# A fused attention and phase-mixing kernel on one core: the loads of the first batch, the angle reduction and the written-out order are changed

## The chip, the cores and the metric

The kernel runs on one core of one Trainium2 chip, in one launch. The metric is the device time of that core in microseconds. Five instruction streams take part: PE (TensorE, matmuls; PEld is its weight load), DVE (VectorE), ACT (ScalarE), POOL (GpSimd) and SP (SyncE, which only issues transfers). SP, ACT and POOL each have a queue of DMA transfers; all queues feed the same 16 DMA engines.

## The reference

The inputs `q`, `k`, `v` are 8 batches x 8 heads x 576 positions x 64 channels in float32. Attention without a softmax is followed by a normalisation, and its result `x` (8 x 576 x 512) goes through a layer that mixes positions with two 576 x 576 matrices and channels with one 512 x 512 matrix:

```python
kv = np.einsum('bhsd,bhse->bhde', k, v)
out = np.einsum('bhsd,bhde->bhse', q, kv)
x = out / sqrt(mean(out * out, axis=-1) + 1e-06) * g_norm    # heads side by side
theta = x @ w_theta
yr = np.einsum('ts,bsd->btd', w_tok_r, x * cos(theta))
yi = np.einsum('ts,bsd->btd', w_tok_i, x * sin(theta))
u = x + yr + yi
return u + np.maximum(u @ w_ch, 0.0)
```

## The kernel before, in words

The 576 positions of a batch are cut into four row tiles of 128 (j = 0 to 3) and a tail of 64 (j = 4), whose two halves of the channels lie above each other so that it fills 128 partitions with half the width. For each batch `b` the work is a chain of small tasks, each of one engine, and each has a short name in the code:

- loads of `k`, `v` (float32, into two buffers each, `kt` and `vt`) and of `q` (cast to float16 on the way, three buffers); each has a part of 512 positions ("heads", rows of 1 KB) and a part of the last 64 ("tail", rows of 256 bytes);
- `kv`: the products of k and v over all positions (L266, 80 small float32 matmuls a batch), copied into block-diagonal `kbd` (`ko`, L286 on ACT or L288 on DVE); `qt`, `qo`: q transposed;
- `raw` (L323), its squares on ACT (`sq`, L345), their sums on DVE (`ss`, L354), the root on POOL (`rt`, L364; for batch 0 on ACT and DVE), `x` on DVE (L386), `xt`, `xc`: x transposed and scaled by g;
- `th` (L451): theta into PSUM. The weights were scaled by 8/(2 pi) in advance, so that theta comes in eighths of a turn. Then `pt` (`whole_turns`, ACT, L467) adds a large number that rounds theta to whole turns; `ar` (`reduce_arg`, DVE, L472) takes the difference to theta, with theta read from PSUM; `ab` (`even_arg`) takes its absolute value (ACT, L480, or DVE on the bits as int32, L482); `si` (L490) and `co` (L497) are the sine of the difference and, by the absolute value and a quarter turn as bias, the cosine, each 512 wide on ACT;
- `z` (DVE, L520; the tail L509): x times both, 1024 wide, into `zm`;
- `y` (L543): the mixing of positions, 8 column tiles in 3 parts each, with weights `wT` that are made once at the start from `w_tok_i` and `w_tok_r` (`wt`: transposes on PE, `wo`: copies); `um` (DVE, L548): u; `ut`, `uo`: u transposed back; `v` (L451): u @ w_ch; `fin` (DVE, L585): the output tile; `st`: its store, from SP.

Nothing is looped at run time, and nothing is scheduled by the framework. `TURNS` is a table of task numbers; `play` walks it and emits each task, so each engine executes its own tasks in the table's order and waits, in order, for what each needs. A `*` picks the second of two engines that a task may run on; `r6` or `a20` are so many idle matmuls on PE (L623), which do no useful work. A queue's transfers start in the order of its issuing engine, and an instruction that waits on SP or POOL holds up all that stands behind it there.

At the start, SP loads k of batch 0, g and theta's weights (float32, into the space of `zm[1]`; four `wg` tasks, three on ACT and one on DVE, scale them into float16 `wth`), then v and k of batch 1. ACT loads v of batch 0. POOL loads q of batch 0, then waits by a one-element copy (`hold`, L232) until the second half of k has landed, loads the two token matrices, waits in the same way for v of batch 1, and loads q of batches 1 and 2 and `w_ch`.

## Time and profile before

| what | value |
|---|---|
| median of 3 runs (lowest, highest) | 214.74 us (213.78, 215.28) |
| the profiled execution: span, first to last instruction | 212.2 us |
| mean granted TensorE clock | 0.988 |
| busy: PE, DVE, ACT, POOL | 199.3, 177.7, 137.2, 75.7 us |
| read from and written to HBM | 33.06 MB, 9.44 MB |

The profiled execution's own time is not listed beside its span; the span lies 2.5 us under the median of the runs (214.74 - 212.2), and that difference stands for what lies around it. Of a row in a view of groups: the line, engine and operation, what it writes and reads, its shape, how often (x), then busy time in us, mean ns of one, and the idle time in front. PE's busy time overlaps from one matmul to the next, so a PE that is busy all the time may still do less than it could.

### The profile page before, as it was taken

What the parts mean: (1) busy time and instruction counts of PE and PEld (TensorE: products, weight loads), DVE (VectorE), ACT (ScalarE), POOL (GpSimd) and SP (SyncE); (2) the same over time, 40 slices, a digit from 0 to 9 for tenths busy, and PEclk for the clock granted to TensorE, in tenths of its full rate; (3) what the DMA queues carried; (4) which work ended last, traced back from release to release, by engine and by line L of the source; (5) the groups of instructions that cost most, each with busy time, mean ns of one, the idle gap of its engine ahead of it and who ended that gap; (6) DMA issues with size and microseconds to landing.
All of it is one profiled execution on the core that took longest, in us unless ns stands there. A gap on an engine that the chain in (4) does not pass through costs nothing.

```text
span 212.2 us, 5401 instructions
## 1 busy us (share of the span) xinstructions
PE 199.3 (94%) x2152; PEld 137.2 (65%) x2152; DVE 177.7 (84%) x379; ACT 137.2 (65%) x268; POOL 75.7 (36%) x74
## 2 busy tenths in 40 slices
PE   7699699999999999989999999999999999999992
PEld 2246368886766785857776567867567856665850
DVE  6007998979999989999999998877997999899652
ACT  2006798658993776845999878574765998466030
POOL 6400070058814750654874550313325630400000
PEclk9889999999999999999999999999999999999998
DMA  6999999993999993999989928956583587563315
GB/s 202 269 298 245 246 249 191 303 313 103 131 226 357 287 240 77 240 229 238 287 259 224 227 29 223 321 140 175 140 183 94 145 121 228 123 90 124 111 55 170
DMA packets 68712, 41.98 MB, mean 198 GB/s; under 512 B 37584, under 2 KB 63824, under 8 KB 68688
## 3 DMA queue, kind: packets, MB, share of 16 engines
q1 hardware_dynamic: 53440, 33.89, 62.0%
q0 software_dynamic: 13664, 6.57, 23.6%
q10 hardware_dynamic: 1584, 1.18, 1.8%
q8 instruction: 17, 0.28, 0.5%
...
HBM read 33.06 MB, written 9.44 MB: 200 GB/s over the span
## 4 chain that ended last, share of the span: by engine, by line
PE 50%; DVE 31%; DMA 7%; ACT 4%; POOL 4%; issue 3%; DVEq 0%; POOLq 0%; ACTq 0%
PE y L543 19%; PE th L451 8%; PE v L451 6%; DVE ot L585 5%; PE kv L266 5%; DVE ss L354 5%; DVE arg L472 4%; POOL rt L364 4%; DVE zm L520 4%; DMA vt<-in_v_dram 3%; DVE zt L509 3%; PE idle L623 3%; DVE x L386 3%; DVE wn L548 2%; DVE kbd L288 2%
## 5 line engine op out<-in xcount | busy, mean ns | idle before, releaser
L364 POOL TENSOR_TENSOR rt<-ss,mhalf 128x8 f32<-128x8 f32 (+1 forms) x35 | 53.6, 1537 | 85.3 <-DVE ss L354 85.0
L543 PE MATMUL y<-wT,zm 128*128 128x320 f16 (+1 forms) x512 | 78.5, 286 | 1.7 <-DVE zm L520 0.9
L543 PEld LDWEIGHTS <-zm 128*128 128x128 f16 x512 | 48.1, 98 | 18.3 <-issue 2.6
L548 DVE SCALAR_TENSOR_TENSOR wn<-y,gcol,xT 128x320 f16<-128x320 f32 (+1 forms) x64 | 31.4, 511 | 2.8 <-PE y L543 2.6
L451 PE MATMUL th<-wth,xT 128*128 128x512 f16 x128 | 32.2, 379 | 0.8 <-DVE kbd L288 0.8
L467 ACT ACTIVATE arg<-th 128x512 f32<-128x512 f32 (+1 forms) x40 | 21.7, 552 | 16.2 <-PE th L451 15.6
L451 PE MATMUL v<-wch,wn 128*128 128x512 f16 x128 | 31.7, 379 | 0.0
L497 ACT ACTIVATE sc<-arg,quarter 128x512 f16<-128x512 f32 (+1 forms) x40 | 26.4, 672 | 0.8 <-DVE arg L482 0.7
L472 DVE SCALAR_TENSOR_TENSOR arg<-arg,th 128x512 f32<-128x512 f32 (+1 forms) x40 | 24.9, 628 | 1.4 <-ACT arg L467 1.3
L490 ACT ACTIVATE sc<-arg 128x512 f16<-128x512 f32 (+1 forms) x40 | 22.9, 583 | 4.3 <-DVE arg L472 4.2
L386 DVE TENSOR_TENSOR x<-raw,rt 128x512 f16<-128x512 f32 x32 | 21.8, 685 | 3.9 <-POOL rt L364 3.5
L266 PE MATMUL kv<-vt,kt 128*64 128x64 f32 x640 | 21.2, 224 | 2.0 <-DMA vt<-in_v_dram 2.0
L354 DVE TENSOR_REDUCE ss<-sqb 128x8 f32<-128x520 f32 x32 | 21.8, 687 | 0.9 <-ACT sqb L345 0.7
L345 ACT ACTIVATE sqb<-raw 128x512 f32<-128x512 f32 x32 | 18.6, 597 | 6.1 <-PE raw L323 5.9
L266 PEld LDWEIGHTS kv<-vt,kt 128*64 128x64 f32 x640 | 19.7, 138 | 4.1 <-issue 2.9
L520 DVE TENSOR_TENSOR zm<-x,sc 128x1024 f16<-128x1024 f16 x32 | 21.7, 685 | 0.6 <-ACT sc L497 0.5
L585 DVE SCALAR_TENSOR_TENSOR ot<-v,us 128x512 f32<-128x512 f32 (+1 forms) x28 | 16.8, 609 | 3.3 <-PE v L451 2.6
L451 PEld LDWEIGHTS <-wn 128*128 128x128 f16 x128 | 11.9, 98 | 10.8 <-issue 0.2
L451 PEld LDWEIGHTS <-xT 128*128 128x128 f16 x128 | 11.7, 98 | 10.8 <-issue 1.4
L543 PE MATMUL y<-wT,zt 128*128 128x320 f16 (+1 forms) x64 | 18.3, 286 | 0.1
L286 ACT COPY us<-ups 128x512 f16<-128x512 f16 (+1 forms) x16 | 8.6, 542 | 13.2 <-PE ups L281 11.7
L480 ACT ACTIVATE arg<-arg 128x512 f32<-128x512 f32 (+1 forms) x25 | 14.1, 575 | 2.8 <-DVE arg L472 2.8
...
## 6 DMA issues: line engine op xcount, KB each, us to landing
...
vt<-in_v_dram SPq DMA_DIRECT2D x7, 1024.0 KB, 9.7
kt<-in_k_dram SPq DMA_DIRECT2D x7, 1024.0 KB, 9.8
...
kt<-in_k_dram SPq DMA_DIRECT2D x8, 128.0 KB, 8.6
zm<-in_moe_w_theta_dram SPq DMA_DIRECT2D x1, 1024.0 KB, 11.7
```

The costliest lines, as they stand in the source:

```text
L266: nc.tensor.matmul(t[i * D:(i + 1) * D, hp - lo, :], ks, vs, start=(hp == lo and j == 0), stop=(hp == lo + n - 1 and j == NT - 1),)
L354: nc.vector.reduce_sum(out=ss[:], in_=sq_sb.pop((b, j))[:], axis=AXX)
L364: nc.gpsimd.tensor_tensor(out=rt[:], in0=ss[:], in1=mhalf[:, 0:h], op=ALU.pow)
L386: nc.vector.tensor_tensor(out=x_pair[b, p][:, :, a * HC:(a + 1) * HC].rearrange("p t (h e) -> p h t e", e=D), in0=r[:].rearrange("p (h t e ...
L451: nc.tensor.matmul(t[:], piece(kc), w[:, kc, :], start=first, stop=last)
L472: nc.vector.scalar_tensor_tensor(out=arg[:, 0, :], in0=arg[:, 1, :], scalar=MAGIC, in1=th_ps.pop((b, j))[:], op0=ALU.subtract, op1=ALU.sub ...
L490: nc.scalar.activation(out=sc[:, 0, :], in_=arg_sb[b, j][:, 0, :], func=AFT.Sin, bias=0.0, scale=-TURN * SHRINK,)
L497: nc.scalar.activation(out=sc_sb[b, j][:, 1, :], in_=arg_sb.pop((b, j))[:, 1, :], func=AFT.Sin, bias=quarter[:], scale=-TURN * SHRINK,)
L520: nc.vector.tensor_tensor(out=dst, in0=x.unsqueeze(1).broadcast_to((P, 2, w)), in1=sc[:], op=ALU.mult)
L543: nc.tensor.matmul(t[:, 0:hi - lo], s, wT[:, w, lo:hi], start=n == 0, stop=n == len(z) - 1)
L548: nc.vector.scalar_tensor_tensor(out=uTb[b % NUT][:, c, lo:hi], in0=y_ps.pop((b, h, c))[:, 0:hi - lo], scalar=gcol[:, 0:1], in1=xTb[b % NX ...
L585: nc.vector.scalar_tensor_tensor(out=ot[:].rearrange("p (c s) -> p c s", s=P), in0=v_ps.pop((b, j))[:].rearrange("p (c s) -> p c s", s=P), ...
```

## The change

1. Batch 0's v goes on SP's queue too, and the order there is first half of v, first half of k, both tails, second halves. A `hold` can now stand anywhere in the table (`p` on POOL: a one-element copy; `s` on SP: a one-element transfer); it reads an element of a loaded buffer (`landed`), so the issuing engine waits for that load before it issues the next. There are 12 on POOL and 8 on SP.
2. Theta's weights are loaded by POOL with a cast to float16, unscaled. The staging in `zm[1]` and the four `wg` tasks go.
3. The angle: `pt` (`turns`, ACT) writes theta times 2^20/(2 pi) as int32; `pq` (`quarter_on`) writes the same plus a quarter turn beside it, on ACT from PSUM (25 of 40) or on DVE from the first half (15); `ar` (`wrap`, DVE) shifts both halves left by 12 bits in one instruction of 1024 int32, which drops whole turns; `si` (`sines`, ACT) takes one sine of 1024. `ab` and `co` go.
4. A store may go on POOL's queue: 11 full tiles and 6 tail halves do. There are four output buffers instead of three.
5. `TURNS` is new throughout, with new choices of engine: of the 36 instructions of `ko`, 4 instead of 18 are on DVE (the others on ACT), of the full `qo` 2 instead of 8; of the full `xc`, 10 instead of 5 are on DVE, of the full `xo` 3 instead of 1. Idle matmuls: 28 instead of 36.

SP's queue from its start (`kt`, `vt` are the buffers of k and v, with the buffer's number; 128x4x256 is one half of the heads, 64x8x64 the tail). Before:

```order
L187 DMA kt0_64<-in_k_dram 128x4x256 x2
L229 DMA gcol_102<-in_g_norm_dram 64x1
L193 DMA kt0_64<-in_k_dram 64x8x64
L229 DMA gcol_102<-in_g_norm_dram 64x1
L223 DMA zm1_77<-in_moe_w_theta_dram 128x4x512
L187 DMA vt1_67<-in_v_dram 128x8x256
L193 DMA vt1_67<-in_v_dram 64x8x64
L187 DMA kt1_65<-in_k_dram 128x8x256
L193 DMA kt1_65<-in_k_dram 64x8x64
```

And now (L624 is a hold):

```order
L190 DMA vt0_66<-in_v_dram 128x4x256
L190 DMA kt0_64<-in_k_dram 128x4x256
L196 DMA vt0_66<-in_v_dram 64x8x64
L196 DMA kt0_64<-in_k_dram 64x8x64
L232 DMA gcol_104<-in_g_norm_dram 64x1
L190 DMA vt0_66<-in_v_dram 128x4x256
L190 DMA kt0_64<-in_k_dram 128x4x256
L232 DMA gcol_104<-in_g_norm_dram 64x1
L624 DMA gate1_101<-qh0_68 1x1
L196 DMA vt1_67<-in_v_dram 64x8x64
L196 DMA kt1_65<-in_k_dram 64x8x64
L190 DMA kt1_65<-in_k_dram 128x8x256
```

v of batch 0 came in, theta's weights went out, and batch 1 stands behind a hold on the second half of q; its tails lead, and its v (behind one more hold) comes last.

POOL's queue from its first load (`qh`, `qe`: q's heads and tail; `wn1`, `wnt1`: the imaginary token matrix, `wn0`, `wnt0`: the real one). Before:

```order
L203 DMA qh0_68<-in_q_dram 128x4x256 x2
L209 DMA qe0_71<-in_q_dram 64x4x64 x2
L232 COPY gate_103<-kt0_64 1x1
L215 DMA wn1_86<-in_moe_w_tok_i_dram 128x2304
L220 DMA wnt1_88<-in_moe_w_tok_i_dram 64x576
L215 DMA wn0_85<-in_moe_w_tok_r_dram 128x2304
L220 DMA wnt0_87<-in_moe_w_tok_r_dram 64x576
L232 COPY gate_103<-vt1_67 1x1
L203 DMA qh1_69<-in_q_dram 128x8x256
```

And now, from the second half of q on (L626 is a hold; ahead of these rows stand the first half of q and two holds, on the first half of v and the tail of k):

```order
L206 DMA qh0_68<-in_q_dram 128x4x256
L212 DMA qe0_71<-in_q_dram 64x4x64
L626 COPY gate1_101<-qh0_68 1x1
L212 DMA qe0_71<-in_q_dram 64x4x64
L626 COPY gate0_100<-vt0_66 1x1
L223 DMA wnt1_88<-in_moe_w_tok_i_dram 64x576
L218 DMA wn1_86<-in_moe_w_tok_i_dram 128x2304
L626 COPY gate0_100<-kt0_64 1x1
L226 DMA wth_90<-in_moe_w_theta_dram 128x4x512
L218 DMA wn0_85<-in_moe_w_tok_r_dram 128x2304
L223 DMA wnt0_87<-in_moe_w_tok_r_dram 64x576
L626 COPY gate0_100<-kt1_65 1x1
```

Theta's weights now stand between the two token matrices, and what follows waits for k of batch 1.

DVE in the angles of batch 0 (`arg` is the angle, `xT` x transposed, `wT` the token weights). Before:

```order
L472 SCALAR_TENSOR_TENSOR arg_381<-arg_381,th_357 128x512
L421 TENSOR_SCALAR xT0_82<-xps_396,gcol_102 128x4x128
L288 COPY wT_89<-wps_390 128x576
L482 TENSOR_SCALAR arg_381<-arg_381 128x512
L288 COPY wT_89<-wps_412 128x576
```

And now:

```order
L466 TENSOR_SCALAR arg_392<-arg_392 128x512
L472 TENSOR_SCALAR arg_392<-arg_392 128x1024
L466 TENSOR_SCALAR arg_401<-arg_401 128x512
L472 TENSOR_SCALAR arg_401<-arg_401 128x1024
L410 TENSOR_SCALAR xT0_82<-xps_410,gcol_104 128x4x64
```

DVE no longer reads theta in PSUM; L466 adds the quarter turn, L472 shifts. The diff, cut to its core:

```diff
--- before.py
+++ after.py
@@ TURNS @@
-0 2 6 r6 7 8 a5 3 5 4 r1 9 32 11 1 10 13 25 26 18 19 20 23 24 a20 38 52 53* 39 33 44 60 34 35 21 22
+r5 a1 3 0 6 r7 26 a1 r3 4 27 1 28 29 a3 30 46 a1 47 31* 38 39* p1 r7 40 41 42 p2 7 10 5 2 48 32 33
...
-def play(tasks, turns, idle):
+def play(tasks, turns, idle, hold):
...
+        if turn[0] in "sp":
+            hold({"s": "SP", "p": "POOL"}[turn[0]], int(turn[1:]))
             continue
         t = tasks[int(turn.rstrip("*"))]
@@ -126,10 +128,10 @@
     eps = 1e-6
-    UNIT = 8.0
-    MAGIC = 1.5 * 2.0 ** 23 * UNIT
-    TURN = 2.0 * math.pi / UNIT
-    SHRINK = 1.0 - 1e-6
+    FINE = 20
+    PER_TURN = 2.0 ** FINE / (2.0 * math.pi)
+    QUARTER = 2.0 ** (FINE - 2)
+    ANGLE = 2.0 * math.pi / 2.0 ** 32 * (1.0 - 1e-6)
     const = ctx.enter_context(tc.tile_pool(name="const", bufs=1))
     work = ctx.enter_context(tc.tile_pool(name="work", bufs=1))
@@ -137,6 +139,8 @@
+    NARG = 2
+    NOT = 4
@@ -163,16 +167,15 @@
-    wth_s = zm[1][:].rearrange("p j i c -> p j (i c)").bitcast(FP32)
+    gate = {t: const.tile([1, 32], t, name=f"gate{n}") for n, t in enumerate((FP32, FP16))}
-    gate = const.tile([1, 1], FP32, name="gate")
@@ -220,32 +223,18 @@
         nc.gpsimd.dma_start(out=wnt[at][:], in_=w_in[SM:S, :])
     def theta_in():
-        nc.sync.dma_start(out=wth_s, in_=moe_w_theta.rearrange("(kc p) c -> p kc c", p=P))
+        nc.gpsimd.dma_start(out=wth[:], in_=moe_w_theta.rearrange("(kc p) c -> p kc c", p=P))
     def channel_in():
         nc.gpsimd.dma_start(out=wch[:], in_=moe_w_ch.rearrange("(kc p) c -> p kc c", p=P))
     def g_in(lo):
         nc.sync.dma_start(out=gcol[lo:lo + D, :], in_=g_norm.unsqueeze(1))
-
-    def hold_pool(src):
-        nc.gpsimd.tensor_copy(out=gate[:], in_=src)
     def scale_g():
         nc.vector.tensor_scalar(
             out=gcol[:], in0=gcol[:], scalar1=math.sqrt(D), scalar2=None, op0=ALU.mult
         )
-
-    def scale_theta(kc, eng):
-        if eng == "ACT":
-            nc.scalar.activation(
-                out=wth[:, kc, :], in_=wth_s[:, kc, :], func=AFT.Copy, scale=1.0 / TURN
-            )
-        else:
-            nc.vector.tensor_scalar(
-                out=wth[:, kc, :], in0=wth_s[:, kc, :], scalar1=1.0 / TURN, scalar2=None,
-                op0=ALU.mult,
-            )
     PS_TR, PS_RAW, PS_ACC = ("tr", 2), ("raw", 2), ("acc", 4)
     raw_ps, th_ps, y_ps, v_ps, kv_ps, tr_ps = {}, {}, {}, {}, {}, {}
@@ -461,43 +450,36 @@
         dense(t, lambda kc: x_piece(b, j, kc), wth, j)
         th_ps[b, j] = t
-    def whole_turns(b, j):
+    def turns(b, j):
         w, e = (C, "") if full(j) else (HC, "e")
-        arg = work.tile([P, 2, w], FP32, tag="arg" + e, bufs=2, name="arg")
-        nc.scalar.activation(out=arg[:, 1, :], in_=th_ps[b, j][:], func=AFT.Copy, bias=MAGIC)
+        arg = work.tile([P, 2, w], I32, tag="arg" + e, bufs=NARG, name="arg")
+        nc.scalar.activation(out=arg[:, 0, :], in_=th_ps[b, j][:], func=AFT.Copy, scale=PER_TURN)
         arg_sb[b, j] = arg
-    def reduce_arg(b, j):
+    def quarter_on(b, j, eng):
+        arg, t = arg_sb[b, j], th_ps.pop((b, j))
+        if eng == "ACT":
+            nc.scalar.activation(
+                out=arg[:, 1, :], in_=t[:], func=AFT.Copy, scale=PER_TURN, bias=QUARTER
+            )
+        else:
+            nc.vector.tensor_scalar(
+                out=arg[:, 1, :], in0=arg[:, 0, :], scalar1=QUARTER, scalar2=None, op0=ALU.add
+            )
+
+    def wrap(b, j):
         arg = arg_sb[b, j]
-        nc.vector.scalar_tensor_tensor(
-            out=arg[:, 0, :], in0=arg[:, 1, :], scalar=MAGIC,
-            in1=th_ps.pop((b, j))[:], op0=ALU.subtract, op1=ALU.subtract,
-        )
-
-    def even_arg(b, j, eng):
-        arg = arg_sb[b, j]
-        if eng == "ACT":
-            nc.scalar.activation(out=arg[:, 1, :], in_=arg[:, 0, :], func=AFT.Abs)
-            return
         nc.vector.tensor_scalar(
-            out=arg[:, 1, :].bitcast(I32), in0=arg[:, 0, :].bitcast(I32),
-            scalar1=0x7FFFFFFF, scalar2=None, op0=ALU.bitwise_and,
-        )
-
-    def sine(b, j):
+            out=arg[:], in0=arg[:], scalar1=32 - FINE, scalar2=None, op0=ALU.logical_shift_left
+        )
+
+    def sines(b, j):
         w, e = (C, "") if full(j) else (HC, "e")
         sc = work.tile([P, 2, w], FP16, tag="sc" + e, bufs=2, name="sc")
         nc.scalar.activation(
-            out=sc[:, 0, :], in_=arg_sb[b, j][:, 0, :], func=AFT.Sin,
-            bias=0.0, scale=-TURN * SHRINK,
+            out=sc[:], in_=arg_sb.pop((b, j))[:], func=AFT.Sin, bias=0.0, scale=ANGLE,
         )
         sc_sb[b, j] = sc
-
-    def cosine(b, j):
-        nc.scalar.activation(
-            out=sc_sb[b, j][:, 1, :], in_=arg_sb.pop((b, j))[:, 1, :], func=AFT.Sin,
-            bias=quarter[:], scale=-TURN * SHRINK,
-        )
     def z_make(b, j):
         x, sc = x_sb[b, j], sc_sb.pop((b, j))
@@ -590,14 +572,15 @@
         )
         ot_sb[b, j] = ot
-    def store(b, j, hh):
+    def store(b, j, hh, e):
         ot = ot_sb[b, j]
+        queue = nc.gpsimd if e == "POOL" else nc.sync
         if full(j):
-            nc.sync.dma_start(
+            queue.dma_start(
                 out=out[b, 0:SM, :].rearrange("(p j) c -> p j c", j=NJ)[:, j, :], in_=ot[:]
             )
         else:
-            nc.sync.dma_start(
+            queue.dma_start(
                 out=out[b, SM:S, hh * HC:(hh + 1) * HC],
                 in_=ot[hh * TL:(hh + 1) * TL, :],
             )
@@ -622,6 +605,26 @@
         for _ in range(n):
             nc.tensor.matmul(t[:], ident[:], fill[:], start=True, stop=True)
+    landed = [
+        lambda: kt[0][0:1, 0:1], lambda: vt[0][0:1, 0:1],
+        lambda: kt[0][0:1, H * NJ * D:H * NJ * D + 1], lambda: vt[0][0:1, H * NJ * D:H * NJ * D + 1],
+        lambda: kt[0][0:1, HH * NJ * D:HH * NJ * D + 1], lambda: vt[0][0:1, HH * NJ * D:HH * NJ * D + 1],
+        lambda: qh[0][0:1, 0, 0:1], lambda: qh[0][0:1, HH, 0:1], lambda: qe[0][TL:TL + 1, 0, 0:1],
+        lambda: wth[0:1, 0, 0:1], lambda: wn[1][0:1, 0, 0:1], lambda: wnt[1][0:1, 0:1],
+        lambda: wn[0][0:1, 0, 0:1], lambda: wnt[0][0:1, 0:1],
+        lambda: kt[1][0:1, 0:1], lambda: vt[1][0:1, 0:1],
+    ]
+    held = []
+
+    def hold(eng, n):
+        src = landed[n]()
+        held.append(n)
+        dst = gate[src.dtype][:, len(held):len(held) + 1]
+        if eng == "SP":
+            nc.sync.dma_start(out=dst, in_=src)
+        else:
+            nc.gpsimd.tensor_copy(out=dst, in_=src)
+
     tasks = []
     def add(name, eng, fn, deps=(), takes=()):
@@ -643,7 +646,7 @@
-    k0, v0 = halves_of_0(nc.sync, "SP", kt[0], k, "k"), halves_of_0(nc.scalar, "ACT", vt[0], v, "v")
+    k0, v0 = halves_of_0(nc.sync, "SP", kt[0], k, "k"), halves_of_0(nc.sync, "SP", vt[0], v, "v")
@@ -652,14 +655,11 @@
-    wth_in = add("load wth", "SP", theta_in)
-    got["wth"] = [add(f"wg {kc}", "DVE|ACT", lambda e, kc=kc: scale_theta(kc, e), [wth_in])
-                  for kc in range(NKC)]
-    hold = add("hold p", "POOL", lambda: hold_pool(kt[0][0:1, (H - 1) * NJ * D:(H - 1) * NJ * D + 1]), [k0[1]])
-    got["tok", 0] = [add("load toki", "POOL", lambda: token_in(moe_w_tok_i, 1), [hold]),
-                     add("load tokie", "POOL", lambda: token_tail_in(moe_w_tok_i, 1), [hold])]
-    got["tok", 1] = [add("load tokr", "POOL", lambda: token_in(moe_w_tok_r, 0), [hold]),
-                     add("load tokre", "POOL", lambda: token_tail_in(moe_w_tok_r, 0), [hold])]
+    got["wth"] = [add("load wth", "POOL", theta_in)]
+    got["tok", 0] = [add("load toki", "POOL", lambda: token_in(moe_w_tok_i, 1)),
+                     add("load tokie", "POOL", lambda: token_tail_in(moe_w_tok_i, 1))]
+    got["tok", 1] = [add("load tokr", "POOL", lambda: token_in(moe_w_tok_r, 0)),
+                     add("load tokre", "POOL", lambda: token_tail_in(moe_w_tok_r, 0))]
@@ -673,11 +673,8 @@
-            got["hold"] = [add("hold v", "POOL", lambda: hold_pool(vt[1][0:1, 0:1]), k_[2:3])]
-            got["wch"] = [add("load wch", "POOL", channel_in, got["hold"])]
+            got["wch"] = [add("load wch", "POOL", channel_in)]
-        if b == 2:
-            old = old + got["hold"]
@@ -776,17 +773,16 @@
-            pt = add(f"pt{w} {b} {j}", "ACT", lambda b=b, j=j: whole_turns(b, j), [th], [("arg" + w, 2)])
-            ar = add(f"ar{w} {b} {j}", "DVE", lambda b=b, j=j: reduce_arg(b, j), [pt])
-            ab = add(f"ab{w} {b} {j}", "DVE|ACT", lambda e, b=b, j=j: even_arg(b, j, e), [ar])
-            si = add(f"si{w} {b} {j}", "ACT", lambda b=b, j=j: sine(b, j), [ar, sine_ready],
+            pt = add(f"pt{w} {b} {j}", "ACT", lambda b=b, j=j: turns(b, j), [th], [("arg" + w, NARG)])
+            pq = add(f"pq{w} {b} {j}", "ACT|DVE", lambda e, b=b, j=j: quarter_on(b, j, e), [pt])
+            ar = add(f"ar{w} {b} {j}", "DVE", lambda b=b, j=j: wrap(b, j), [pq])
+            si = add(f"si{w} {b} {j}", "ACT", lambda b=b, j=j: sines(b, j), [ar, sine_ready],
-            co = add(f"co{w} {b} {j}", "ACT", lambda b=b, j=j: cosine(b, j), [ab, si])
-                    [co, *of("y", b - NZ), *(got["wth"] if b == 1 else [])],
+                    [si, *of("y", b - NZ)],
-            pt.readers, th.readers, si.readers = [ar, ab, si, co], [pt, ar], [co, z]
+            pt.readers, th.readers, si.readers = [pq, ar, si], [pt, pq], [z]
@@ -850,10 +846,11 @@
-                      [("ot" + w, 3)])
+                      [("ot" + w, 3 if w else NOT)])
-            fin.readers = [add(f"st{w} {b} {j}{hh}", "SP", lambda b=b, j=j, hh=hh: store(b, j, hh), [fin])
+            fin.readers = [add(f"st{w} {b} {j}{hh}", "SP|POOL",
+                               lambda e, b=b, j=j, hh=hh: store(b, j, hh, e), [fin])
@@ -862,13 +859,13 @@
-        nc.vector.memset(quarter[:], math.pi / 2)
+        nc.vector.memset(quarter[:], 0.25)
-        play(tasks, TURNS, idle)
+        play(tasks, TURNS, idle, hold)
```

101 lines of the change are left out of this document (52 added, 49 removed), and 3 rows, old and new, of the table TURNS.

## The prediction

> **What bounds the kernel now.** I read the page first (busy shares, and the chain of waits that ended last), then cut the span where the look of the rows changes.
>
> ```profile
> PE 199.3 (94%) x2152; PEld 137.2 (65%) x2152; DVE 177.7 (84%) x379; ACT 137.2 (65%) x268; POOL 75.7 (36%) x74
> ...
> PE 50%; DVE 31%; DMA 7%; ACT 4%; POOL 4%; issue 3%; DVEq 0%; POOLq 0%; ACTq 0%
> ```
>
> ```profile
> 0.00:33.40 33.40, 27.45 (x240) 15.07 (x240) 19.09 (x53) 15.81 (x35) 10.13 (x22) 0.95 1.09 248
> 33.40:207.40 174.00, 171.25 (x1905) 121.77 (x1906) 157.52 (x324) 121.04 (x233) 65.53 (x52) 1.00 0.85 190
> 207.40:212.20 4.80, 0.64 (x12) 0.37 (x12) 1.12 (x2) 0.37 (x1) 0.00 (x0) 0.84 0.45 148
> ```
>
> The windows give, after the length, busy time of PE, PEld, DVE, ACT, POOL, then clock, DMA share and GB/s. The middle one is the machine at work: PE busy 171.25 of 174 us, DVE 157.52 (90.5%); they lean on each other, and little can be taken out of PE. The first 33 us are different: the DMA share is 1.09, that is, full, and much of PE's 27.45 us is filler.
>
> ```profile
> 8.37 0.69 PE L266 MATMUL kv<-vt,kt 128*64 128x64 f32 x16 [2.00 <-DMA vt<-in_v_dram]
> 8.98 6.18 PE L623 MATMUL idle<-fill,ident 128*128 128x512 f16 x20
> ...
> 24.96 1.03 PE L451 MATMUL th<-wth,xT 128*128 128x512 f16 x4
> ...
> 33.42 1.39 PE L266 MATMUL kv<-vt,kt 128*64 128x64 f32 x40
> 34.74 0.41 PE L613 MATMUL wps<-ident,wn 128*128 128x128 f16 x4
> 35.24 0.42 PE L613 MATMUL wps<-ident,wn 128*128 128x128 f16 x4
> ```
>
> PE's first product waits for data until 8.37, then twenty filler matmuls pass the time to 15, theta starts at 24.96, and batch 1's product at 33.42. From there PE hardly rests. So the change can gain in two places: the start, where transfers decide, and the long middle, where DVE does.
>
> **The start.** What has landed when, by the transfers issued in the first 14 us:
>
> ```profile
> kt<-in_k_dram SPq DMA_DIRECT2D x1, 1024.0 KB, 18.6
> ...
> vt<-in_v_dram ACTq DMA_DIRECT2D x1, 128.0 KB, 13.4
> ```
>
> ```profile
> 2.55 0.75 ACTq L193 DMA_DIRECT2D vt<-in_v_dram  x1
> ```
>
> ```profile
> 12.26 0.62 SPq L187 DMA_DIRECT2D kt<-in_k_dram  x1
> ```
>
> Batch 0's last piece, v's tail, was issued at 2.55 and took 13.4: 15.9 us. Batch 1's k landed at 12.26 + 18.6 = 30.9. By then, from the shapes, 3.54 MB had been read for batch 0's q, k, v, 1.05 for theta's weights, 2.65 for the token matrices and 2.23 for batch 1's k and v without k's tail: 9.47 MB in 29.4 us from 1.5, or 0.32 MB a us.
>
> In the new order batch 0 comes alone: 3.54 MB at that rate are there at 1.5 + 11.0 = 12.5, some 3 us sooner, though short rows and holds that leave a queue empty may cost one of these. Theta's weights now come behind the imaginary token matrix: 5.92 MB, 19.9 us if batch 1 gets nothing in between, more like 22 since its tails share the engines; theta can start there instead of at 24.96. But batch 1's product needs all 9.60 MB, and these are the same bytes as before: 1.5 + 9.60/0.32 = 31.3, and the hold that frees q of batch 1 when k has landed lets a fourth transfer in beside the rest of v, for which I add 1.0: **32.3 us**. PE is there sooner: theta at 22, then (durations in the rows below) 1.03 + 0.60 + 0.42 + 0.69 + 1.06 = 3.8 to the end of the first angles, and z, one more tile and two copies of token weights on top, some 3: about 29. So it waits for v. What it has done by then is more than before, by the two groups of transposes that stood at 34.74 and 35.24 (0.50 from start to start, 1.0) and three parts of the position mixing (three matmuls each, by the rows of about the same width in PE's stream an estimate of 0.3): 1.9 us. Start: 33.4 - 32.3 + 1.9 = **3.0 us gained**. Bounds: 5.0 if v is there at 30.3, 0.7 if q of batch 1 takes its whole 3.3 us out of v's time. Putting v on SP instead of ACT costs nothing by itself: SP has no other work there, and its holds wait for loads that the next ones would only delay.
>
> **The angles and the copies.**
>
> ```profile
> L467 ACT ACTIVATE arg<-th 128x512 f32<-128x512 f32 (+1 forms) x40 | 21.7, 552 | 16.2 <-PE th L451 15.6
> ...
> L497 ACT ACTIVATE sc<-arg,quarter 128x512 f16<-128x512 f32 (+1 forms) x40 | 26.4, 672 | 0.8 <-DVE arg L482 0.7
> L472 DVE SCALAR_TENSOR_TENSOR arg<-arg,th 128x512 f32<-128x512 f32 (+1 forms) x40 | 24.9, 628 | 1.4 <-ACT arg L467 1.3
> L490 ACT ACTIVATE sc<-arg 128x512 f16<-128x512 f32 (+1 forms) x40 | 22.9, 583 | 4.3 <-DVE arg L472 4.2
> ```
>
> The same six instructions as one tile's view has them, with the least, the median and the longest of each in ns; with 32 of 512 and 8 of 256 columns, the median is that of 512 and the least is one of 256:
>
> ```profile
> L467 ACT ACTIVATE arg<-th x40: 363/597/609, 26.4 to 190.1; 128x512 f32<-128x512 f32 x32, 128x256 f32<-128x256 f32 x8
> L472 DVE SCALAR_TENSOR_TENSOR arg<-arg,th x40: 410/678/690, 27.3 to 190.9; 128x512 f32<-128x512 f32 x32, 128x256 f32<-128x256 f32 x8
> L490 ACT ACTIVATE sc<-arg x40: 403/622/652, 28.4 to 192.3; 128x512 f16<-128x512 f32 x32, 128x256 f16<-128x256 f32 x8
> L497 ACT ACTIVATE sc<-arg,quarter x40: 491/710/732, 29.4 to 193.7; 128x512 f16<-128x512 f32 x32, 128x256 f16<-128x256 f32 x8
> L480 ACT ACTIVATE arg<-arg x25: 399/621/644, 36.4 to 193.3; 128x512 f32<-128x512 f32 x19, 128x256 f32<-128x256 f32 x6
> L482 DVE TENSOR_SCALAR arg<-arg x15: 283/418/428, 28.7 to 191.8; 128x512 int32<-128x512 int32 x13, 128x256 int32<-128x256 int32 x2
> ```
>
> And the copies on DVE that move:
>
> ```profile
> L288 DVE CAST kbd<-kv x18: 276/418/428, 18.6 to 114.4; 64x256 f16<-64x256 f32 x14, 64x128 f16<-64x128 f32 x4
> L288 DVE COPY us<-ups x12: 280/414/418, 51.9 to 205.9; 128x512 f16<-128x512 f16 x7, 128x256 f16<-128x256 f16 x5
> L288 DVE COPY qT<-qps x11: 291/415/425, 16.1 to 89.2; 128x512 f16<-128x512 f16 x8, 128x256 f16<-128x256 f16 x3
> ```
>
> ```profile
> L421 DVE TENSOR_SCALAR xT<-xps,gcol x7: 298/476/484, 26.5 to 100.0; 128x512 f16<-128x512 f16 x5, 128x256 f16<-128x256 f16 x2
> ```
>
> No shift is in the trace. Its nearest row is the bitwise operation on int32 (L482), 283 ns for 256 and 418 for 512, 0.527 an element: 688 ns for 1024 if a shift goes as fast. At the pace of the difference it replaces (L472, 410 and 678, 1.05 an element) it is 1214. I take 688, since engine, operation class and type are the same. DVE: 32 x 0.688 + 8 x 0.418 = 25.4 for 24.9; adds 12 x 0.418 + 3 x 0.283 = 5.9 for 13 x 0.418 + 2 x 0.283 = 6.0. The copies matter more: 14 casts of `kbd` leave (at 0.418, -5.9), 6 of q (at 0.415, -2.5), some 8 scalings of x come (at 0.476, +3.8), and net three small copies go (at 0.414, -1.2). DVE: **-5.4**, 3% of 177.7. ACT: one sine of 1024 is 622 + 2 x 219 = 1060 (slope from 256 to 512), 32 x 1.060 + 8 x 0.622 = 38.9 for 22.9 + 26.4; second conversions 25 x 0.552 = 13.8 for 19 x 0.621 + 6 x 0.399 = 14.2 of absolute values (L480). ACT: -10.8 from the angles; the copies that arrive are about balanced by scalings that leave.
>
> What that is worth in the middle I take from the chain: DVE 31% of 212.2 is 65.8 us, of which 5.4/177.7 is 2.0; ACT 4%, 10.8/137.2 of it 0.7. Against it stand POOL's stores:
>
> ```profile
> L364 POOL TENSOR_TENSOR rt<-ss,mhalf 128x8 f32<-128x8 f32 (+1 forms) x35 | 53.6, 1537 | 85.3 <-DVE ss L354 85.0
> L209 POOL DMA_DIRECT2D qe<-in_q_dram x16 | 10.1, 643 | 0.0
> L203 POOL DMA_DIRECT2D qh<-in_q_dram x9 | 8.2, 916 | 1.5 <-PE qps L281 1.1 <-issue 0.3
> ```
>
> 11 x 0.92 + 6 x 0.64 = 14.0 us of issuing that SP did for nothing now stand in POOL's stream, between the roots that DVE waits for. POOL sits idle most of the time, so most of it hides; by POOL's 4% it would be 8.5 x 14.0/75.7 = 1.6 on the path, and I take half, 0.8. The holds on POOL are one-element copies; those far into the program read buffers loaded long before. Sum 2.0 + 0.7 - 0.8 = 1.9, of which the first 33.4 us hold 19.09/177.7: **1.7 us gained**, between 5.4 (every saved us of DVE is on the path) and a loss. The end is the same work in another order, a full last tile for a half: nothing.
>
> **Sum:** 212.2 - 3.0 - 1.7 = 207.5 of span, and 2.5 around it (214.74 - 212.2): **210.0 us**, 2.2% under the median.
>
> **Rivals.** *The bytes decide, and nothing else moves* (chance 0.19). Batch 1's v lands at 34.6 behind q, the start keeps 0.7, and DVE's saving drowns in new waits: 212.2 - 0.7 + 2.5 = 214.0. For it: the first 33 us have a full DMA share, and the bytes are the same. Against: batch 0 gets 3 us.
>
> *The later holds starve batch 3* (0.07). A hold on SP waits for q of batch 3 before k and v of batch 3 and v of batch 4 are issued, 3.4 MB or 10.6 us at 0.32. POOL issues that q after batch 1's last root; if it lands near 58, k's tail lands near 70, where PE wants it at about 68, then waits again for a k held behind it; I put 5 us on it: 210.0 + 5 = 215.0. It decides when q lands after 56.
>
> *The shift runs at one element a cycle's pace, 1215 ns* (slower, 0.05). Extra DVE work 32 x 0.53 + 8 x 0.26 = 19.0, of which 35 of 40 tiles in the middle carry 16.6. DVE there would have 157.5 - 4.8 + 16.6 = 169.3 us; at today's 90.5% that takes 187 instead of 174: 212.2 - 3.0 + 13 + 2.5 = 224.7. It decides from the point at which the saving at the start is eaten, some 0.25 us per shift more, or 0.94 us. Against it: L482's slope.
>
> *Shifts and adds wait for POOL's roots* (slower, 0.05). 55 integer instructions on DVE meet a POOL that is busy 65.53 of 174 us: 21 of them, half a root each (0.8), 17 us, and again about 225.
>
> ```profile
> 85.17 1.64 POOL L364 TENSOR_TENSOR rt<-ss,mhalf 128x8 f32<-128x8 f32 x1 [6.89 <-DVE ss L354]
> ```
>
> ```profile
> 86.13 0.42 DVE L482 TENSOR_SCALAR arg<-arg 128x512 int32<-128x512 int32 x1
> ```
>
> Against it: this int32 operation began and ended inside a root and took its usual 0.42. The Trainium skill's page "SBUF — State Buffer", section "Who interferes with whom", states this rival as a rule: a DVE `tensor_scalar` in a two-port mode and a GpSimd instruction lock each other out, and the second to start waits for all of the first. By that rule the time is that of this rival; the trace does not agree in the one place above, so I leave it a small chance.
>
> **How the numbers follow.** My forecast has 0.64, the rivals 0.19, 0.07, 0.05 and 0.05. A measurement tells about 1% from no change here, so the bounds are 212.6 and 216.9. Faster: 0.62 from the forecast and 0.02 from the first rival, 0.64. Within 1%: 0.02, 0.17 and 0.05, 0.24. Slower: 0.02 from the starved batch and 0.10, 0.12. The low end has 5.0 at the start and some 3 in the middle, 212.2 - 8.0 + 2.5 = 206.7, and 2 below it for waits in the middle that I cannot see now, 204.7; the high end is 215.5, just over the second rival. The forecast's own range is 206.7 to 212.6.
>
> **What would show it.** Right: first product near 6.5 to 7, theta near 22, batch 1's product at 31 to 33 after a wait for v, the shift near 0.69, the long sine near 1.06, DVE busy some 172, ACT some 127, no long wait of DVE for POOL. Wrong: batch 1's product after 34; a shift over 0.9; kv of batch 3 waiting for k; roots that start late behind stores on POOL.

## The result, and the profile after

| kernel | median, us (lowest to highest) | against before, 95% interval |
|---|---|---|
| before, on the same chip | 215.01 (213.78 to 215.59) | 1 |
| changed | 225.18 (224.29 to 225.70) | 1.0487 (1.0442 to 1.0532) |

The change makes the kernel 4.9% slower. 210.0 was forecast, in a range from 204.7 to 215.5; the time lies 9.7 us above its upper end. Some executions of a kernel fall into a slower state; the ratios here and below leave them out, the medians include them. The profiled execution took 225.7, its span is 223.9. The page's busy shares and its chain of waits:

```profile
PE 199.9 (89%) x2144; PEld 139.9 (62%) x2144; DVE 174.0 (78%) x365; ACT 131.2 (59%) x238; POOL 90.6 (40%) x102
...
PE 55%; DMA 16%; issue 8%; DVE 6%; POOL 6%; ACT 3%; SPq 3%; POOLq 0%; DVEq 0%; ACTq 0%
```

DVE and ACT have less to do than before (177.7 and 137.2), as intended, and yet the span is 11.7 longer. In the chain, transfers went from 7% to 16%: the time went to waiting for data, not to work. The windows, cut where PE's rows change (length; busy PE, PEld, DVE, ACT, POOL; granted clock; DMA share; GB/s), say where:

```profile
0.00:34.40 34.40, 28.45 (x251) 16.79 (x251) 19.71 (x51) 18.66 (x37) 10.78 (x28) 0.90 1.00 212
34.40:69.40 35.00, 35.00 (x457) 26.18 (x455) 31.17 (x65) 27.80 (x52) 21.31 (x25) 1.00 1.03 181
69.40:78.40 9.00, 0.10 (x3) 0.08 (x3) 3.99 (x8) 1.09 (x2) 4.29 (x4) 0.78 1.24 274
78.40:86.00 7.60, 4.63 (x82) 4.44 (x84) 0.00 (x0) 0.00 (x0) 0.00 (x0) 0.50 0.71 182
86.00:90.00 4.00, 4.00 (x35) 2.28 (x30) 1.22 (x3) 1.95 (x5) 0.00 (x0) 0.75 0.87 247
90.00:218.70 128.70, 127.75 (x1329) 90.09 (x1327) 117.47 (x241) 81.72 (x144) 53.74 (x47) 1.00 0.83 174
```

Nearly all of the loss lies between 69.4 and 90, where PE is busy 8.7 of 20.6 us. PE does nothing for 9.0 us; then it works at half the clock, and while batch 3's product runs, DVE, ACT and POOL stand still. PE's rows there:

```profile
69.17 0.28 PE L270 MATMUL xps<-ident,x 128*128 128x128 f16 x2
78.35 1.12 PE L255 MATMUL kv<-vt,kt 128*64 128x64 f32 x16 [8.90 <-issue]
82.44 3.68 PE L255 MATMUL kv<-vt,kt 128*64 128x64 f32 x64 [2.97 <-DMA kt<-in_k_dram]
85.91 1.07 PE L443 MATMUL th<-wth,xT 128*64 128x256 f16 x8
```

L255 is batch 3's product of k and v. It waits 8.90 for v and, after 16 matmuls, 2.97 for k's tail. (The profile puts the first wait down to "issue"; the first part of k had landed at 64.0, 5.5 after its issue at 58.52, and in experiment 4 the trace names v for the same wait.) Who was late is SP, whose waits (us in all, times, longest) and rows (start, length) are:

```profile
SPq L624 <- DMA qh<-in_q_dram: 17.5, 2, 11.1
...
SPq L624 <- POOL gate L626: 5.1, 1, 5.1
```

```profile
57.83 0.63 SPq L624 DMA_DIRECT2D gate<-qh  x1
58.52 0.38 SPq L190 DMA_DIRECT2D kt<-in_k_dram  x1
64.10 0.62 SPq L624 DMA_DIRECT2D gate<-wn  x1
64.82 0.67 SPq L196 DMA_DIRECT2D kt<-in_k_dram  x1
65.54 3.47 SPq L190 DMA_DIRECT2D vt<-in_v_dram  x2
69.06 5.28 SPq L196 DMA_DIRECT2D kt<-in_k_dram  x1
```

Two holds stand there, with the first part of k of batch 3 between them. The first waits until 57.83 for q of batch 3, 11.1 us. The second should wait for nothing: it reads the imaginary token matrix, which was there at 20. It waits 5.1 us for L626, a hold of POOL. POOL's rows:

```profile
60.64 3.26 POOL L353 TENSOR_TENSOR rt<-ss,mhalf 128x8 f32<-128x8 f32 x2 [3.56 <-DVE ss L343]
63.87 0.21 POOL L626 COPY gate<-qh 1x1 f16<-1x1 f16 x1
```

That hold comes behind two roots and ends at 64.08; at 64.10 SP goes on. Holds write into a small buffer for each type, each into the cell of its number; these two are the 16th and the 17th, so their float16 cells lie 2 bytes apart in one 4-byte word, and the program makes the write into the one wait for the write into the other (with the cells 4 bytes apart, in experiment 1, this wait of SP for POOL is gone). So v of batch 3 is issued at 65.54, and k's tail, behind v of batch 4, at 69.06, 0.4 us before PE runs out of work.

### The profile page after: what moved, and what is told of

It reads as the page before. It is cut to its first block, busy times and chain, and to the rows that moved or that the text cites. A ratio compares the mean times of both kernels' runs of the same rounds, so it can differ in the third digit from the quotient of the medians.

```text
span 223.9 us, 5370 instructions
## 1 busy us (share of the span) xinstructions
PE 199.9 (89%) x2144; PEld 139.9 (62%) x2144; DVE 174.0 (78%) x365; ACT 131.2 (59%) x238; POOL 90.6 (40%) x102
## 4 chain that ended last, share of the span: by engine, by line
PE 55%; DMA 16%; issue 8%; DVE 6%; POOL 6%; ACT 3%; SPq 3%; POOLq 0%; DVEq 0%; ACTq 0%
PE y L525 23%; PE th L440 10%; DMA kt<-in_k_dram 9%; PE v L440 6%; PE kv L255 6%; DMA wth<-in_moe_w_theta_dram 5%; POOL rt L353 3%; DMA out_dram<-ot 2%; SPq L190 2%; PE raw L312 2%; PE xps L270 2%; PE th L443 2%; ACT sc L479 1%; DVE ss L343 1%; DVE x L375 1%
## 5 line engine op out<-in xcount | busy, mean ns | idle before, releaser
L353 POOL TENSOR_TENSOR rt<-ss,mhalf 128x8 f32<-128x8 f32 (+1 forms) x35 | 56.3, 1648 | 77.0 <-DVE ss L343 77.0
L525 PE MATMUL y<-wT,zm 128*128 128x256 f16 (+1 forms) x512 | 76.3, 286 | 0.3 <-DVE ot L567 0.3
L525 PEld LDWEIGHTS <-zm 128*128 128x128 f16 x512 | 48.3, 98 | 15.2 <-issue 0.9
L479 ACT ACTIVATE sc<-arg 128x1024 f16<-128x1024 int32 (+1 forms) x40 | 38.3, 972 | 8.0 <-DVE arg L472 7.8
L530 DVE SCALAR_TENSOR_TENSOR wn<-y,gcol,xT 128x256 f16<-128x256 f32 (+1 forms) x64 | 31.4, 511 | 5.6 <-PE y L525 5.1
L255 PE MATMUL kv<-vt,kt 128*64 128x64 f32 x640 | 23.7, 235 | 13.2 <-issue 8.9
L456 ACT ACTIVATE arg<-th 128x512 int32<-128x512 f32 (+1 forms) x40 | 22.0, 555 | 19.7 <-PE th L440 16.0
L255 PEld LDWEIGHTS kv<-vt,kt 128*64 128x64 f32 x640 | 22.2, 149 | 14.8 <-issue 11.6
L472 DVE TENSOR_SCALAR arg<-arg 128x1024 int32<-128x1024 int32 (+1 forms) x40 | 25.3, 643 | 1.4 <-ACT arg L462 1.0
L275 ACT CAST kbd<-kv 64x256 f16<-64x256 f32 (+1 forms) x32 | 11.2, 351 | 25.8 <-PE kv L255 25.5
L440 PEld LDWEIGHTS <-wn 128*128 128x128 f16 x128 | 11.7, 99 | 12.0 <-issue 1.8
L440 PEld LDWEIGHTS <-xT 128*128 128x128 f16 x128 | 12.2, 100 | 11.0 <-issue 1.8
L277 DVE COPY us<-ups 128x512 f16<-128x512 f16 (+1 forms) x13 | 4.8, 373 | 15.9 <-PE ups L270 15.9
L579 POOL DMA_DIRECT2D out_dram<-ot x11 | 6.9, 625 | 18.7 <-DVE ot L567 18.7
```

What stands on the lines that cost most here:

```text
L255: nc.tensor.matmul(t[i * D:(i + 1) * D, hp - lo, :], ks, vs, start=(hp == lo and j == 0), stop=(hp == lo + n - 1 and j == NT - 1),)
L353: nc.gpsimd.tensor_tensor(out=rt[:], in0=ss[:], in1=mhalf[:, 0:h], op=ALU.pow)
L440: nc.tensor.matmul(t[:], piece(kc), w[:, kc, :], start=first, stop=last)
L456: nc.scalar.activation(out=arg[:, 0, :], in_=th_ps[b, j][:], func=AFT.Copy, scale=PER_TURN)
L472: nc.vector.tensor_scalar(out=arg[:], in0=arg[:], scalar1=32 - FINE, scalar2=None, op0=ALU.logical_shift_left)
L479: nc.scalar.activation(out=sc[:], in_=arg_sb.pop((b, j))[:], func=AFT.Sin, bias=0.0, scale=ANGLE,)
```

## The experiments

Twelve kernels in three groups; each group ran on one chip with its own runs of the kernel before. "Base" from the second group on is the changed kernel without the seven late holds (experiment 3). The kernel before took 215.01 us beside the changed kernel, and 214.36, 214.94 and 214.58 in the three groups, so a difference of medians across groups is uncertain by some 0.6 us; the ratios to the kernel before take that out, and where the two give different sizes, both stand.

**1. The cells apart.** The 20 holds stay.

```diff
-        held.append(n)
-        dst = gate[src.dtype][:, len(held):len(held) + 1]
+        held.append(src.dtype)
+        at = held.count(src.dtype) * (2 if src.dtype == FP16 else 1)
+        dst = gate[src.dtype][:, at:at + 1]
```

> All 20 holds stay where they are. Only the cells that the float16 holds write are put 4 bytes apart instead of 2, so that SP's hold ahead of batch 4's k tail no longer shares a word with the hold that POOL does just before it, and no longer waits for POOL. Theory A (the changed kernel loses its time because that hold waits for POOL, which is behind two roots: k and v of batches 3 and 4 are issued from 64.8 instead of about 59): they are issued from about 59, batch 3's product starts near 70 instead of 78.4 and 82.4, PE loses 2 us there instead of 12, and the time is 225.2 - 11 = 214, between 211 and 216. Theory B (the hold before it, on q of batch 3, is what is late, since it ends at 57.8): 222 to 225. Theory C (the bytes are late whatever is held): 224 to 226.

219.30, ratio 1.0198 (1.0134 to 1.0263): 5.9 less than the changed kernel (6.2 by the ratios), neither 11 (A) nor 0 to 3 (B). The second hold now starts at 58.28, right behind the load ahead of it, and v of batch 3 is issued at 59.73 instead of 65.54:

```profile
57.12 0.64 SPq L625 DMA_DIRECT2D gate<-qh  x1
57.81 0.38 SPq L190 DMA_DIRECT2D kt<-in_k_dram  x1
58.28 0.62 SPq L625 DMA_DIRECT2D gate<-wn  x1
59.01 0.67 SPq L196 DMA_DIRECT2D kt<-in_k_dram  x1
59.73 2.28 SPq L190 DMA_DIRECT2D vt<-in_v_dram  x2
62.06 2.99 SPq L196 DMA_DIRECT2D kt<-in_k_dram  x1
```

Batch 3's product now starts at 68.71 without a wait: v is there. But after 16 matmuls PE waits 5.92 for k's tail, which was issued at 62.06, behind v of batch 4:

```profile
68.71 0.69 PE L255 MATMUL kv<-vt,kt 128*64 128x64 f32 x16
75.32 3.68 PE L255 MATMUL kv<-vt,kt 128*64 128x64 f32 x64 [5.92 <-DMA kt<-in_k_dram]
```

(The profiled execution took 221.0, more than the median.) So the shared word is real and worth about half. The rest goes with the first hold, by the difference to the next experiment; no run takes out the first hold alone.

**2. Without the two holds.** `s7` and `s10` are SP's holds ahead of k of batch 3 and of batch 4's k tail.

```diff
-359 372 373 s7 279 184
+359 372 373 279 184
...
-360 276 341 s10 488 343
+360 276 341 488 343
```

> SP's two holds ahead of k of batch 3 and of batch 4's k tail are left out; nothing else is changed. Theory A: as in the run with the cells apart, 211 to 216, batch 3's product near 70, since k of batch 3 was in time already. Theory B: only here the time comes back, 210 to 214, and the run with the cells apart stays above 220. Theory C: 224 to 226.

212.59, ratio 0.9907 (0.9871 to 0.9944). 12.6 us come back (12.4 by the ratios), which A and B both allow, and PE has no gap over 0.3 us at batch 3's product. The four loads behind the holds stand in the same order as in the changed kernel.

**3. Without all late holds.** Also out: `p10` and `p6` on POOL, and `s0`, `s3`, and the last `s2` on SP.

```diff
-382 383* 271 269 p10 270 179
+382 383* 271 269 270 179
...
-398* 668 s0 494 366 s3 379
+398* 668 494 366 379
```

> The last seven holds (from the one that POOL does ahead of q of batch 3 on) are left out, on POOL and SP; the first 13 stay. Theory A: 210 to 216, within 1.5 of the run without the two holds, because the others wait for loads that are there. Theory C, or a theory in which the holds keep the queues clear for what is wanted next: over 217.

211.54, ratio 0.9865 (0.9837 to 0.9893): 1.3% faster than before. From experiment 2 the intervals don't tell it apart, so what the other five holds cost is little or nothing. What the holds did to the transfers, in windows (the last two columns are DMA share and GB/s), first of the changed kernel, then without the late holds:

```profile
52.00:56.00 4.00, 4.00 (x105) 3.31 (x103) 3.67 (x8) 3.93 (x8) 3.00 (x4) 1.00 1.03 100
56.00:60.00 4.00, 4.00 (x40) 2.37 (x37) 3.84 (x10) 3.93 (x10) 1.09 (x3) 1.00 0.83 84
```

```profile
52.00:56.00 4.00, 4.00 (x93) 3.10 (x93) 3.88 (x8) 3.93 (x7) 3.00 (x5) 1.00 1.34 281
56.00:60.00 4.00, 3.53 (x48) 2.37 (x46) 3.30 (x8) 3.92 (x9) 1.44 (x2) 1.00 1.49 210
```

While PE was still busy with older work, the queues moved 100 and 84 GB/s instead of 281 and 210: 1.2 MB, more than a batch's v, were not moved in these 8 us and had to come in a burst with q of batches 4 and 5 and a store after 64.

**4. Batch 3 first.** All holds stay; v and k's tail of batch 3 are issued ahead of k's tail and v of batch 4.

In the table, 343 and 342 are v and k's tail of batch 3, 488 and 489 k's tail and v of batch 4.

```diff
-341 s10 488 343 300
+341 s10 343 342 488 300
...
-376 489 342 490 173
+376 489 490 173
```

> All holds stay, the shared word too. Behind the hold, v and k's tail of batch 3 are issued ahead of k's tail and v of batch 4. Theory A: the hold still ends at 64.1, so batch 3's product still starts late, but its last piece lands some 5 us sooner: 219 to 222. Theory D (the order of the four loads behind the hold, and not the hold, is at fault): 211 to 216.

221.61, ratio 1.0344 (1.0315 to 1.0373): 3.6 less (3.1 by the ratios), as A has it. The wait is 5.44 and 1.02 instead of 8.90 and 2.97. The order behind the hold is worth that much; most of the loss is the holds.

**5 and 9. Idle matmuls at the start.** In base, PE stands still four times between 15.2 and 19.5 (0.73, 0.52, 0.90 and 0.57 us), and the granted clock is then 0.50 and 0.67. In run 5 the 13 idle matmuls write PSUM buffers of the kind `a` (`a3` are three), in run 9 of the kind `r`, which nothing else uses there. They stand in five places ahead of tasks that PE waited for; three of these, as run 9 has them:

```diff
-37 43 64 44
+37 43 r3 64 44
...
-70 71 72 73
+70 71 r4 72 73
...
-61 74 127 67
+61 74 r3 127 67
```

> The kernel without the seven late holds, and 13 more idle matmuls on PE, put where PE stood still between 15 and 24 us. Theory K (the start gains little because the granted clock falls to 0.50 from 20 to 25 us and 0.67 to 30 after PE stood still, so that batch 1's product starts at 34.9 though its v landed at 32.9): the clock stays over 0.9 from 20 to 30, the product starts near 33, 1.5 to 2 us less than the 211.5 of the kernel without the late holds: 209.5 to 210. Theory V (what bounds the start is the landing of the loads, the clock only fills waiting time): the product is at 34 or later, and the time is 211 to 212.

> As the run with 13 more idle matmuls between 15 and 24 us, but they write PSUM buffers that nothing else uses there: in that run three of them waited 1.70 us for a buffer that DVE still read, and PE stood still again. Theory K (the clock): no gap of PE over 0.7 us between 14 and 24, granted clock over 0.9 from 20 to 30, batch 1's product near 33, 209.5 to 210. Theory V (the loads): the product at 34 or later, 211 to 212.

Run 5: 213.54, ratio 0.9921 (0.9892 to 0.9950), 0.6% above base (the intervals just touch); PE stood still for 1.70 at 20.9, since three idle matmuls waited for a buffer that DVE still read, and the clock fell all the same. Run 9: 211.26, ratio 0.9827 (0.9797 to 0.9858), the best kernel of the study, 1.7% faster than before, and from base not told apart by the intervals. Base (first fence) and run 9 (second), 20 to 30 us:

```profile
20.00:25.00 5.00, 4.54 (x25) 2.51 (x25) 3.26 (x9) 4.09 (x7) 0.00 (x0) 0.50 1.12 215
25.00:30.00 5.00, 5.00 (x28) 2.74 (x26) 3.32 (x7) 2.80 (x5) 0.00 (x0) 0.67 1.11 310
```

```profile
20.00:25.00 5.00, 4.22 (x38) 2.89 (x39) 3.27 (x10) 4.36 (x8) 0.00 (x0) 1.00 1.13 221
25.00:30.00 5.00, 5.00 (x42) 2.83 (x40) 4.64 (x11) 4.09 (x7) 0.00 (x0) 1.00 1.11 321
```

The clock (third column from the end) is whole in run 9, and PE's matmuls in the same 10 us are 80 instead of 53. Yet 1.4 us are gained at batch 1's product, 33.51 for 34.93: there PE now waits for v, which landed at 33.38:

```profile
33.51 2.55 PE L255 MATMUL kv<-vt,kt 128*64 128x64 f32 x80 [0.80 <-DMA vt<-in_v_dram]
```

So for the start theories K and V are both right, one after the other: first the clock, then the load. K's time, 209.5 to 210, is not reached: of the 1.4 us at the product 0.3 show in the median and 0.8 by the ratios, neither clear of the intervals.

**6. No holds at all.** The 13 early ones are left out too.

> All 20 holds are left out, the 13 early ones too; nothing else. Theory H (the early holds pay, since they keep batch 0's loads clear of the later ones): batch 0 lands 2 to 4 us later, and the time is 2 to 4 over the 211.5 of the kernel without the late holds: 213.5 to 215.5. Rival (all bytes have to come anyway before batch 1's product): 211 to 212.

219.78, ratio 1.0213 (1.0170 to 1.0256), 8.2 more than base (7.5 by the ratios), so theory H has the direction and less than half of the size. The last piece of batch 0's k lands at 20.0 instead of 12.2, and batch 1's product starts at 40.9 instead of 34.9. The early holds pay: at the start the engines have nothing else to do, and later loads that run beside batch 0's make them late.

**7. All stores on SP.** The 17 that were POOL's (a star picks POOL here); the first two:

```diff
-309 301 188* 314 637
+309 301 188 314 637
...
-636 292 194* 505 506
+636 292 194 505 506
```

> The kernel without the late holds, with all stores on SP's queue. If POOL's 14 us of issuing costs what the prediction took, 0.8, the time is 210.7; if it costs nothing, 211.5; if the stores that stand in SP's stream hold up the loads behind them, over 212.5.

214.31, ratio 0.9972 (0.9942 to 1.0001), some 1% over base, the other way than the prediction's price. In its trace DVE and PE wait once, 2.67 and 2.38, near 193: SP needs 4.73 us to issue three stores from 185.04 on, and transposes of u that DVE wants stand behind them. The start of its profiled execution is 1.3 later than base's as well, by the same instructions, and it stays open how much of the 1% is due to that.

**8. Copies on DVE as before.** The engines of `ko` and `qo` from batch 1 on.

A star picks DVE here; three of the places (`ko` of batch 2, two `qo` of batch 3):

```diff
-180* 181 352 353 347
+180* 181 352* 353 347
...
-173 303 501 491 308
+173 303 501* 491 308
...
-361 385 515 312 386
+361 385 515* 312 386
```

> The kernel without the late holds, with the copies of k times v and of q from batch 1 on placed on DVE and ACT as in the kernel before: DVE has 10 copies more (+4.2 us), ACT 10 less. By the prediction's share of the path (31% of the span over 177.7) that is +1.6: 213.1. If every us of DVE is on the path: 215.7. If DVE hides it: 211.5.

222.31, ratio 1.0349 (1.0317 to 1.0380): 10.8 more than base (10.4 by the ratios). A copy of k times v is two instructions, so DVE had 17 more and not 10; its busy time went from 174.2 to 181.1. Even so 6.9 us of DVE cost 10.8. PE's waits in this kernel (in all, times, longest), two of them of kinds that base does not have (its longest wait for `kbd` is 0.7):

```profile
PE xps L270 <- DVE x L375: 2.2, 2, 1.9
PE raw L312 <- ACT kbd L275: 2.0, 3, 1.1
PE raw L312 <- DVE qT L277: 1.9, 1, 1.9
```

**10. Old angles in the new places.** `pt`, `pq`, `ar`, `si` do rounding, difference, absolute value, and two sines.

```diff
-            out=sc[:], in_=arg_sb.pop((b, j))[:], func=AFT.Sin, bias=0.0, scale=ANGLE,
+            out=sc[:, 0, :], in_=arg[:, 0, :], func=AFT.Sin, bias=0.0, scale=-TURN * SHRINK,
...
+            out=sc[:, 1, :], in_=arg[:, 1, :], func=AFT.Sin, bias=quarter[:],
```

> The kernel without the late holds, with the angles worked out as in the kernel before (rounding, difference from PSUM, absolute value, two sines), in the new order's places; theta's weights stay unscaled, so the angle is 2 pi/8 times theta, which changes the output and not the work. DVE has as much to do (24.9 + 6.0 us for 25.3 + 5.9), ACT 11 more. The prediction took 0.7 for ACT: 212.2. If ACT hides it: 211.5. If the longer chain from theta to z (a second sine and an absolute value, some 0.5 us more for each tile) is on the path: 213.5 or more.

226.81, ratio 1.0563 (1.0532 to 1.0593): 15.3 over base. The first two theories are out; the third, the longer chain, gave only a lower bound. DVE has as much to do as in base (173.5 for 174.2), ACT 7.5 more (139.2 for 131.7). ACT's absolute values now wait for differences on DVE; in this kernel and, for the sine and the shift, in base:

```profile
ACT arg L471 <- DVE arg L463: 18.4, 14, 2.5
```

```profile
ACT sc L478 <- DVE arg L471: 7.9, 10, 2.3
```

In the chain that ended last, ACT has 12% of the span instead of 1%, and DVE 22% instead of 5%.

**11. New angles alone.** In the kernel before, `pt` converts, `ar` adds the quarter turn, `ab` shifts, `co` takes the sine.

```diff
+        nc.vector.tensor_scalar(
+            out=arg[:], in0=arg[:], scalar1=32 - FINE, scalar2=None, op0=ALU.logical_shift_left
+        )
```

> The kernel before, with its loads and its order, and the new angles alone: conversion to int32, quarter turn (25 on ACT, 15 on DVE), one shift of 1024, one sine of 1024. ACT has 11 us less, DVE as much. By the prediction's share 0.7 less than before: 214.2. If ACT is hidden: 214.9, the same. If shifts and POOL's roots hold each other up: over 217.

231.19, ratio 1.0760 (1.0717 to 1.0803), 16.6 over before. The first two theories are out; the third has the direction, but its reason is not in the trace: the shift's median is 0.684, as it is in the changed kernel (0.683). ACT's wait for DVE's angles, in this kernel and in the changed one:

```profile
ACT sc L499 <- DVE arg L489: 27.8, 18, 3.4
```

```profile
ACT sc L479 <- DVE arg L472: 7.8, 10, 2.1
```

ACT has 8.1 us less to do than before (129.1 for 137.2), DVE 0.9 more (178.6 for 177.7). But the sine now waits for a shift that the old order puts late among DVE's instructions, 18 times, up to 3.4 us, and what is queued behind that sine on ACT waits too. One case in the trace goes through to PE: at 166.04 two sines start 2.98 late, and the mixing of positions at 169.60 has waited 2.61 for the z made from them. ACT's share of the chain goes from 4% to 13%.

**12. Quarter turns on ACT.** The 11 `pq` that are on DVE from batch 1 on; the first two:

```diff
-260 172 261* 262 265
+260 172 261 262 265
...
-657 407 401* 495 496
+657 407 401 495 496
```

> The kernel without the late holds; the 11 quarter turns that DVE adds from batch 1 on go to ACT, from PSUM: DVE has 4.3 us less (9 x 0.417 + 2 x 0.28), ACT 6.1 more. Theory M (DVE's load sets the pace of the middle: 17 copies more, 6.9 us, cost 10.8): 4.3 less saves 4 to 7, 205 to 207.5. By the prediction's share, 1.6 less: 210. Theory P (it is the place of those copies that cost, since PE waits for each, and not the load of DVE): 211 to 212.5.

212.06, ratio 0.9870 (0.9836 to 0.9904), not told apart from base: theory P's range, and against theory M. In the trace, which is of the slowest of the six executions (215.75), DVE is busy 3.3 less than in base (170.9 for 174.2) and ACT 4.2 more (136.0 for 131.7). A gain on DVE that ACT's extra work ate up is not ruled out.

## Why the prediction was wrong, step by step

**The step that failed** is the one that costs SP's new order at nothing: "its holds wait for loads that the next ones would only delay". It was written of the start, and the sum has no term for SP's later holds at all. It is so of the early holds (experiment 6: without them 8 us more), and wrong of the two ahead of batch 3's loads. Taking out these two gives back 12.6 of the 225.2; without all late holds the kernel takes 211.5, 1.5 over the forecast. The mechanism stood among the rivals, with the place and the condition: "It decides when q lands after 56"; it landed at 57.8. Its price was 5, and its chance 0.07. Three things were not in it. One is the second hold: it reads a matrix that lay there, and yet it waited 5.1 for POOL through a shared word (worth some 6 us, experiment 1). Then v of batch 3, which stands behind both, was late and not only k's tail, so PE waited 8.90 before the first matmul. And PE came back at a clock of 0.50: batch 3's 80 matmuls took 4.80 with the waits left out (1.12 + 3.68), where batch 1's took 2.55, and the mean clock was 0.75 from 86 to 90. For each hold that the table puts into a queue, the question that had to be asked was not only what it waits for but what would have been transferred meanwhile.

**The start** was priced at 3.0 gained. Batch 1's product starts at 34.45 instead of 33.42, with the 1.9 us of work done ahead as forecast: 0.9 gained. v landed at 33.58 and not at 32.3, 1.3 late; what made it late stays open. Theta, too, started at 23.86 and not near 22. PE, forecast to wait there for v, came 0.9 after it. That part was not in the sum at all: the clock, 0.50 from 20 to 25. PE stood still 2.7 of the 5 us before (2.32 busy), where the new order has no idle matmuls (its last ends at 13.6). In the 3.4 us right before the drop PE was busy 1.37 in the changed kernel (16.36 to 19.77) and 1.64 in base (14.64 to 18.05); in the kernel before, 2.31 of 3.42 (19.50 to 22.92) were followed by no drop. The Trainium skill's page "TensorE: Matmul & The Clock Gate", section "What's actually happening", has the clock at half after an idle window of some 3.4 us and whole after a busy one; the rows agree with half and whole (0.50, 1.00), the values between them being means over a stretch, and four short gaps sufficed here, none over 0.90.

**The instructions** cost what was estimated from their neighbours. One tile's view of the changed kernel (least, median, longest in ns):

```profile
L456 ACT ACTIVATE arg<-th x40: 381/597/621, 25.8 to 201.2; 128x512 int32<-128x512 f32 x32, 128x256 int32<-128x256 f32 x8
L472 DVE TENSOR_SCALAR arg<-arg x40: 414/683/860, 27.5 to 204.6; 128x1024 int32<-128x1024 int32 x32, 128x512 int32<-128x512 int32 x8
L479 ACT ACTIVATE sc<-arg x40: 614/1057/1107, 28.6 to 205.3; 128x1024 f16<-128x1024 int32 x32, 128x512 f16<-128x512 int32 x8
```

The shift takes 683 (688 forecast), the long sine 1057 (1060). Added up by rows, DVE's instructions take 5.3 less than before and ACT's 9.5, close to the 5.4 and 10.8 forecast; but busy time, in which instructions that overlap count once, fell by 3.7 and 6.0. The rival of a shift at 1215 is out. The 2.5 that the sum adds around the span is 1.8 in the profiled execution (225.7 - 223.9); it compared a median with another execution's span.

**Shifts against roots.** This rival fails in size: 17 us were forecast for it. Some roots are longer than the median:

```profile
L353 POOL TENSOR_TENSOR rt<-ss,mhalf x35: 1037/1637/2217, 41.4 to 191.5; 128x8 f32<-128x8 f32 x28, 128x4 f32<-128x4 f32 x7
```

The longest root is 2.22 where 1.64 is the median, the longest shift 0.86; all roots together took 56.3 instead of 53.6. DVE waited for POOL's roots 2.0 us in the whole program (1.8 + 0.2), where it was 4.7 before (3.5 + 1.2). The rule of an exclusive lock, which the prediction cites, shows at most as a few tenths on a root or a shift.

**The middle** was priced at 1.7. Base is 2.8 under before (211.54 for 214.36 on its chip); by the profiles its product of batch 1 starts at 34.93, so that the start, with 1.9 ahead, gave 0.4, and the middle some 2.4. The sum was near by luck, since the way to it was not sound. It took DVE's share of the chain, so much of the path for each us of load. Experiment 8 contradicts that: 6.9 us more of DVE cost 10.8. Experiment 12 gives it no support: 3.3 less saved nothing, with 4.2 more on ACT. Experiments 10 and 11 have about as much work as their bases on DVE, and cost 15.3 and 16.6. The reading that fits all four is that in this kernel, where each engine works down a written list, what counts is whether an instruction's inputs are there when its turn comes. It is argued from the waits in the traces; no run tests it by itself.

**Stores on POOL** were priced at 0.8 lost. Experiment 7 has it the other way, without settling how much.
